# Attention with maxout FFN on one core: loads, bias, score groups and order changed

## The chip, the cores and the metric

The kernel runs on one core of a Trainium2 chip. The metric is the device time of one execution in microseconds. Engines are named as in the profile: PE is TensorE (PEld its weight loads), DVE is VectorE, ACT is ScalarE, POOL is GpSimd, SP is SyncE, whose sequencer here issues nearly all DMAs. An ending q (SPq, ACTq) means that engine's instruction queue. L12 is line 12 of the kernel before.

## The reference

Attention over 4 batches, 8 heads, 768 positions of 64 elements, with a mask and a bias, then a maxout feed-forward layer over the 3072 tokens (512 wide, hidden 768):

```
keep = (column < 8) | (0 <= row - column < 96)
dist = 96 where the column is global and not local, else |row - column|
scores = q k^T / 8 - slope[h] * dist, -1e9 where not keep;  slope[h] = 2 ** -(h + 1)
x = softmax(scores) v
out = max(x w1, x w2, x w3) w_out
```

q, k, v and the weights are fp32 in memory; the output is fp32.

## The kernel before

The 3072 tokens are 24 tiles T of 128 rows, six to a batch. A row tile only needs its own 128 positions, the 128 before it and the 8 global ones, so a tile has two sets of 128 keys (`ds`), the first tile of a batch (T = 0, 6, 12, 18) one. Inside a set, even and odd positions are split (`e`). The order of all work is written out by hand in `SCHEDULE`, a list of units; each engine executes its share of the units in that order, and an instruction waits in its engine's queue for what it needs. A unit is a letter and numbers:

- `l n.s` loads q (s = 0) or k (s = 1) of tiles 2n and 2n+1 (`load_part`, L156), 512 KB in fp32. For `short_rows` (L149; all of n >= 6, and k of n < 3) the descriptors are rows of 512 bytes in one DMA, otherwise rows of 2 KB in two DMAs of 256 KB. `v n` loads v (L171, 512-byte rows), `w`, `o` the weights.
- `c n.s.how` casts such a part to bf16 (L179); how = 0, 1, 2 is ACT, DVE, POOL. `x n.s.how` transposes it into `qkT` (L243): how 2, 3 by 8 matmuls into one PSUM tile and one copy (L282, L285), 6 to 8 by 16 small matmuls (64 rows each) into two and two copies (L261, L266/L268), 9 by DMA (L252). `C`, `Y`, `V` cast and rearrange v into the tiles `vo`, `ve`, `vf`; `G` puts the global keys into place; `Z` (L207) gathers the first key tile of a batch into `kf`.
- `S T.g.how` (L293) computes the scores of four heads g of a tile, by matmuls of 64 rows each, two row halves z side by side, into the PSUM tile `sp`, and ACT's exponential (L317) into `P`. With how = 1 (tiles 0 to 3 and one group of tile 4) the bias is added first by two matmuls of an identity with the table `bias` (L299), which `B h` prepares (L322). With how = 0 DVE multiplies `P` by the table `wmask` afterwards (`M`, L334), which `K h` prepares by ACT.
- `A T.how` multiplies P by v (L360), normalizes and writes `xb` (L373); `T T.how` transposes xb into `xT` (L376): how 0, 1 by four matmuls (L411), 6 to 8 by eight small ones (L401), 4 by DMA (L381). Twelve tiles use PE, twelve DMA.
- `F c.f.j` (L417) is one of three products of 128 hidden units for a chunk c of tokens (chunks of 4, 2, 2, 4, 4, 4, 4 tiles), four matmuls into one of three PSUM buffers `h`; j = 0 is copied by ACT (L429), j = 1, 2 are max'ed by DVE (L431, L433) into `ht`. `W`, `Q` cast the weights. `O` (L451) is the output product of a tile, `E` (L456) that of the last chunk.
- `D` (L498) issues n dummy matmuls of 512 columns (`wp`, L504): 12 before the first data, five more spread over the first 22 us.

The first k part is issued by ACT's queue before ACT's table load, the first q part by SP's (L507, L508). Two units of SP's queue are always issued in their order, so a DMA transposition that waits for `xb` holds up the loads behind it.

Of the kernel before, what the change touches and what calls it, by code (L numbers as in the profile page):

```python
# [12 lines left out]
FP32 = mybir.dt.float32  # L13
# [17 lines left out]
    T3.8 V4.2 W0.1.2 S4.1.0 D7.1 G4.0 w0.2 F0.1.0 F0.0.0 S5.1.0 c3.0.1 x3.0.6 M4.1 w1.0 W1.0.0
    S5.0.0 F0.1.1 W0.2.2 F0.1.2 v2 C2.0.0 C2.1.0 W2.0.1 F0.0.1 F0.0.2 M5.0 F0.3.0 F0.2.0 M5.1 Y2.1.1
    V5.1 F0.5.0 w1.1 W1.1.0 W2.1.1 F0.4.0 A4.1 A5.0 F0.5.1 T4.0 F0.4.1 w1.2 W1.2.0 l3.1 T5.1 F0.2.1
    F0.2.2 l4.0 c4.0.1 W2.2.0 F0.5.2 c3.1.0 x3.1.7 Z1.0 F0.4.2 F1.0.0 F1.2.0 l4.1 c4.1.1 S7.0.0
    S6.1.0 l5.0 x4.0.6 l5.1 o0 F1.0.1 F1.0.2 c5.0.1 M7.0 F1.3.0 F1.4.0 F1.4.1 o2 c5.1.1 x4.1.7
    S6.0.0 S7.1.0 G7.0 v3 F1.2.1 F1.2.2 F1.3.1 Q2.1 F0.3.1 M7.1 Q0.0 F1.5.0 F1.5.1 S8.0.0 x5.0.7
    S8.1.0 G8.1 C3.0.2 C3.1.1 Y4.0.1 F0.3.2 F1.5.2 A7.0 F1.4.2 F1.1.0 M6.0 x5.1.6 v5 o1 Q1.0 v4
    S9.0.0 S9.1.0 l7.0 l6.1 C5.0.1 C5.1.0 F1.1.1 F1.3.2 Y3.1.1 M8.0 F1.1.2 T7.0 v6 l6.0 M6.1 v7
    Y3.0.1 M9.0 O0.2.1 l7.1 C4.0.0 O0.0.0 G9.0 V8.1 A6.1 c7.0.1 M8.1 c6.1.1 x6.1.9 O0.3.0 C4.1.0
    Y4.1.1 O0.1.1 Y5.1.0 S10.1.0 T6.8 V9.1 M9.1 S10.0.0 O1.0.0 A8.1 M10.1 T8.4 F2.0.0 x7.0.9 G10.0  # L40
    F2.4.0 c6.0.0 l8.1 v9 l9.1 F2.0.1 F2.1.0 M10.0 F2.0.2 S11.0.0 c7.1.0 Y5.0.1 x6.0.6 S11.1.0 V10.1
    F2.1.1 M11.0 F2.4.1 C6.0.0 A9.0 F2.2.0 V11.1 l9.0 O1.1.1 S13.1.0 x7.1.6 S13.0.0 G13.0 M11.1
# [16 lines left out]
    O5.3.1 F6.1.1 F6.0.0 F6.0.1 F6.0.2 O5.0.1 F6.2.0 F6.2.1 F6.3.2 O5.2.0 F6.2.2 F6.1.2 F6.5.2 E
    D6.0  # L60
"""


@with_exitstack
def kernel(
# [13 lines left out]
    nc = tc.nc  # L79
# [13 lines left out]
    sizes = [4, 2, 2, 4, 4, 4, 4]  # L93
# [31 lines left out]
    rbq = persist.tile([128, 3, 128], FP32, name="rbq")  # L125
# [449 lines left out]
```

## Time and profile before

| | us |
|---|---|
| device time, median of 3 runs | 176.63 (176.61 to 176.70) |
| span of the profiled execution, first to last instruction | 174.9 |
| the profiled execution's own device time | not listed apart; the median is 1.7 above its span |
| PE / DVE / ACT / POOL busy | 169.3 / 132.5 / 120.1 / 14.3 |

A page of the profile gives busy times, the span in slices, the chain of work that ended last (followed back from the last instruction, at each step to what released it), and groups of instructions with their mean duration. The chain can also be listed in order of time: start, length, engine, output tile, line. In a table by stages each engine has its busy time and its count of instructions.

### The profile page before, as it was taken

To read this page: it belongs to the slowest core of one execution; us is meant where nothing else is said; L and a number is where in the kernel's file an instruction comes from. 1 tells how busy PE (TensorE), PEld (TensorE's weight loads), DVE (VectorE), ACT (ScalarE), POOL (GpSimd) and SP (SyncE) were. 2 spreads that over 40 slices of the span, in tenths; PEclk is the share of its full clock that TensorE was granted. 3 is DMA by queue.
4 is the path that set the end of the run, shared out by engine and by line. 5 is a ranking of instruction groups with operands and counts; after the bars stand their busy time and mean duration, and the time that the engine had idled before them with its cause. 6 is when DMAs were issued, how large, how long until landed. Compare 5 with 4: busy or idle time off the path is not lost.

```text
span 174.9 us, 4233 instructions
## 1 busy us (share of the span) xinstructions
PE 169.3 (97%) x1683; PEld 93.0 (53%) x1683; DVE 132.5 (76%) x288; ACT 120.1 (69%) x188; POOL 14.3 (8%) x25
## 2 busy tenths in 40 slices
PE   6999999999999999999999999999999999999992
PEld 2445654658684587754545545544455544444451
DVE  6668859889999999998978769995569873444510
ACT  6989999789988999999948977345594413121132
POOL 5269250000100000000000000000000000000000
PEclk9999999999999999999999999999999999999999
DMA  4999999999999999976999997563101750031205
GB/s 137 347 302 335 359 350 383 385 380 312 309 282 265 298 289 228 292 213 193 257 195 185 304 233 172 166 133 60 54 10 30 105 171 0 0 119 36 89 27 213
DMA packets 55507, 35.92 MB, mean 205 GB/s; under 512 B 18368, under 2 KB 47936, under 8 KB 55488
## 3 DMA queue, kind: packets, MB, share of 16 engines
q1 hardware_dynamic: 54304, 35.07, 73.9%
q10 hardware_dynamic: 1184, 0.59, 1.3%
q8 instruction: 13, 0.21, 0.5%
q14 instruction: 6, 0.05, 0.1%
HBM read 25.17 MB, written 6.29 MB: 180 GB/s over the span
## 4 chain that ended last, share of the span: by engine, by line
PE 94%; ACT 2%; DVE 1%; issue 1%; ACTq 0%; DVEq 0%
PE h L424 53%; PE po L439 18%; PE sp L306 7%; PE op L360 6%; PE wp L504 4%; PE tpr L261 2%; PE sp L299 2%; PE xtp L411 1%; ACT qkT L268 1%; ACT wo L496 1%; PE oph L360 1%; ACT P L317 1%; PE xtr L401 0%; PE tpp L282 0%; DVE qkT L285 0%
## 5 line engine op out<-in xcount | busy, mean ns | idle before, releaser
L424 PE MATMUL h<-xT,w 128*128 128x512 bf16 (+1 forms) x504 | 100.8, 349 | 0.0
L424 PEld LDWEIGHTS <-w 128*128 128x128 bf16 x504 | 46.7, 98 | 40.7 <-ACT w L493 0.6
L317 ACT ACTIVATE P<-sp 128x1024 bf16<-128x1024 f32 (+1 forms) x48 | 44.0, 956 | 9.2 <-PE sp L306 9.1
L429 ACT CAST h<-h 128x512 bf16<-128x512 f32 (+1 forms) x42 | 21.9, 531 | 22.1 <-PE h L424 22.1
L439 PE MATMUL po<-wo,ht 128*128 128x512 bf16 (+2 forms) x156 | 34.1, 363 | 0.0
L431 DVE TENSOR_TENSOR h<-h,h 128x512 bf16<-128x512 bf16 (+1 forms) x42 | 25.2, 605 | 10.9 <-PE h L424 8.9
L433 DVE TENSOR_TENSOR ht<-h,h 128x512 bf16<-128x512 bf16 (+1 forms) x42 | 25.5, 609 | 6.3 <-PE h L424 5.0
L334 DVE TENSOR_TENSOR P<-P,wmask 128x1024 bf16<-128x1024 bf16 x33 | 22.0, 684 | 2.0 <-ACT P L317 1.9
L439 PEld LDWEIGHTS <-ht 128*128 128x128 bf16 x156 | 14.3, 98 | 15.1 <-DVE ht L433 0.2
L448 ACT COPY ost<-po 128x512 f32<-128x512 f32 (+2 forms) x16 | 8.8, 553 | 15.8 <-PE po L439 15.3
L373 DVE TENSOR_TENSOR xb<-op,rz 128x512 bf16<-128x512 f32 x22 | 15.2, 692 | 0.8
L360 PEld LDWEIGHTS <-P 128*128 128x128 bf16 x352 | 13.4, 97 | 4.4 <-issue 0.7
L306 PE MATMUL sp<-qkT 64*128 64x128 bf16 x320 | 14.3, 218 | 0.1
L306 PEld LDWEIGHTS <-qkT 64*128 64x128 bf16 x320 | 9.3, 94 | 8.2 <-issue 5.1
L448 DVE COPY ost<-po 128x512 f32<-128x512 f32 (+1 forms) x10 | 6.5, 647 | 8.4 <-PE po L439 8.4
L188 DVE CAST qkp<-rawp 128x1024 bf16<-128x1024 f32 x12 | 8.2, 687 | 1.7 <-DMA rawp<-in_k_dram 1.6
L504 PE MATMUL wp<-zeros 128*128 128x512 bf16 x17 | 7.1, 559 | 1.5 <-DVE zeros L518 1.4
L188 ACT CAST qkp<-rawp 128x1024 bf16<-128x1024 f32 x8 | 8.4, 1050 | 0.0
L268 ACT COPY qkT<-tpr 128x512 bf16<-128x512 bf16 x12 | 6.6, 588 | 1.0 <-PE tpr L261 1.0
L268 DVE COPY qkT<-tpr 128x512 bf16<-128x512 bf16 x6 | 4.0, 688 | 3.9 <-PE tpr L261 3.9
L372 DVE RECIPROCAL rz<-op 128x8 f32<-128x8 f32 x22 | 4.4, 199 | 2.5 <-PE op L360 2.3
L360 PE MATMUL op<-vo,P 128*128 128x65 bf16 x128 | 5.4, 193 | 0.3 <-issue 0.3
(84 smaller groups left out, 127.9 us busy)
## 6 DMA issues: line engine op xcount, KB each, us to landing
rawv<-in_v_dram SPq DMA_DIRECT2D x12, 512.0 KB, 7.0
out_dram<-ost SPq DMA_DIRECT2D x23, 256.0 KB, 2.4
rawp<-in_k_dram SPq DMA_DIRECT2D x8, 512.0 KB, 5.9
rawp<-in_q_dram SPq DMA_DIRECT2D x12, 256.0 KB, 5.8
wst<-in_moe_w_dram SPq DMA_DIRECT2D x3, 1024.0 KB, 11.5
rawp<-in_q_dram SPq DMA_DIRECT2D x6, 512.0 KB, 6.2
wst<-in_moe_w_dram SPq DMA_DIRECT2D x3, 512.0 KB, 8.5
rawp<-in_k_dram SPq DMA_DIRECT2D x6, 256.0 KB, 8.6
```

The lines of the kernel that those rows point to most:

```text
L188: copies[how](qk, src)
L306: nc.tensor.matmul(sp[:, z, i, ds], k_cols(T, hsl, jp, ds), q_cols(T, hsl, jp), start=not how, stop=True, skip_group_check=True)
L317: nc.scalar.activation(dst, src, AF.Exp, bias=0.0, scale=scale)
L334: nc.vector.tensor_mul(P, P, wmask[:, g, :, 0:2])
L360: nc.tensor.matmul(o, P[:, i, ds], vs[ds][:, h], start=(ds == 0), stop=(ds == len(vs) - 1), skip_group_check=True)
L373: nc.vector.tensor_tensor(out=x.rearrange("p (g h) d -> p g h d", g=2), in0=o4[:, :, :, 0:64], in1=rz[:, :, :, None].to_broadcast([128, 2, ...
L424: nc.tensor.matmul(ps, w123[f // 2][:, dm, j, (f % 2) * 128:(f % 2) * 128 + 128], xT[c][:, dm], start=(dm == order[0]), stop=(dm == order[ ...
L429: nc.scalar.copy(h01, ps)
L431: nc.vector.tensor_max(h01s[c, f], h01s[c, f], ps)
L433: nc.vector.tensor_max(ht[c][:, f], h01s[c, f], ps)
L439: nc.tensor.matmul(po, ht[c][:, f, tt * 128:(tt + 1) * 128], wo[:, f, cols], start=(f == 0), stop=(f == NF - 1))
L448: copy(ost, po)
```

## The change

- q and k of tiles 0 to 11 all come in rows of 2 KB (`SHORT` is empty). `load_part` takes the queue: 0 SP, 1 ACT, 2 one half on each. The first k is split over SP and ACT, the first q goes by ACT, both as units of the schedule; on ACT they follow the table load and the activation `tiny`.
- The bias is added by four matmuls per group, each of an identity scaled by one head's slope (`slope_id`, prepared by `B`, seven on POOL) with one unscaled distance table `rbqb` in bf16. The group g of heads is now formed as 2i + g.
- The first tile of a batch reads its keys straight from `qkT` by two matmuls of 64 output rows each; `kf` and `Z` go.
- `U T` is both score groups of a tile; all tiles from 6 on use it.
- The v tiles are slices of one tile `vall`, whose ones are set by one memset. Casts can be split over two engines (how 3 to 5) and `Y` can copy by DMA (how 3).
- The schedule is new. In counts: of the x transpositions 11 use 16 small matmuls (13 before), 3 use eight large ones (1), 10 DMA (10); T uses PE for tiles 0 to 3 and DMA for the other 20; q/k casts on ACT/DVE/POOL and split are 3/7/11/3 (8/12/4/0), v casts 4/6/14 (10/9/5), Y and V have 23 units on POOL (4); biased score groups are 8 (9); dummies are seven at the start and five after E; of the three wo casts two are on DVE (one). Instructions: DVE 290 to 252, ACT 192 to 168, POOL 30 to 77.

The new order at its beginning, and around chunk 1:

```
D5.6 D13.1 l0.1.2 c0.1.1 l0.0.1 K5 K2 c0.0.3 x0.1.2 B7.2 B4.2 B3.1 x0.0.6 K4 B5.2 B1.2 K0 S1.1.1
B0.2 l1.1 c1.1.1 B6.2 B2.2 S1.0.1 G1.0 x1.1.3 l1.0 S0.1.1 v0 c1.0.2 x1.0.7 v1 C1.0.1 S0.0.1
...
W2.1.1 W1.1.0 A5.0 A4.1 F0.5.1 F0.2.1 w1.2 W2.2.0 F0.3.1 W1.2.2 l4.0 c4.0.5 M7.1 F0.4.1 F0.3.2
v3 U6.0 M6.0 T5.4 x4.0.7 M6.1 C3.1.1 Y3.1.1 F0.5.2 C3.0.2 Y3.0.2 F0.2.2 T4.4 A7.0 F1.0.0 A6.1
F1.1.0 F1.5.0 F1.1.1 l4.1 c4.1.2 x4.1.7 F0.4.2 U8.0 G8.0 l5.0 c5.0.2 x5.0.6 F1.5.1 F1.1.2 F1.5.2
v5 C5.0.1 F1.2.0 F1.2.1 l5.1 c5.1.5 F1.4.0 F1.4.1 F1.3.0 v4 C4.1.1 x5.1.7 o0 Q0.1 U9.0 F1.2.2
```

The code:

```diff
...
+SIZES = [4, 2, 2, 4, 4, 4, 4]
+SHORT = []
...
-    rbq = persist.tile([128, 3, 128], FP32, name="rbq")
...
     wmask = persist.tile([128, 2, 4, 3, 128], BF16, name="wmask")
-    bias = persist.tile([128, 2, 2, 2, 3, 128], BF16, name="bias")
-    vo_first = [persist.tile([128, 2 * H * 65], BF16, name=f"vof{i}") for i in range(2)]
-    vo_next = [persist.tile([128, 2 * H * 65], BF16, name=f"vo{i}") for i in range(2)]
-    ve = [persist.tile([128, 2 * H * 65], BF16, name=f"ve{i}") for i in range(2)]
-    vf = [persist.tile([128, H * 65], BF16, name=f"vf{i}") for i in range(2)]
-    kf = persist.tile([128, NP, 2, 64], BF16, name="kf")
+    rbqb = persist.tile([128, 3, 128], BF16, name="rbqb")
+    slope_id = persist.tile([128, H, 128], BF16, name="slope_id")
+    vall = persist.tile([128, 14 * H * 65], BF16, name="vall")
+    vparts = [vall[:, i * H * 65:(i + 1) * H * 65] for i in range(14)]
+    pairs = [vall[:, 2 * i * H * 65:2 * (i + 1) * H * 65] for i in range(6)]
+    vo_first, vo_next, ve, vf = pairs[0:2], pairs[2:4], pairs[4:6], vparts[12:14]
     w123 = [persist.tile([128, 4, 3, 256], BF16, name=f"w123_{i}") for i in range(3)]
...
     def heads(ap):
...
+    queues = (nc.sync, nc.scalar)
     def short_rows(n, s):
-        return n >= 6 or (s == 1 and n < 3)
+        return n >= 6 or (n, s) in SHORT
...
-    def load_part(n, s):
+    def load_part(n, s, how=0):
...
         b, t0 = divmod(2 * n, NT)
+        src = (q, k)[s][b, :, t0 * 128:(t0 + 2) * 128, :]
         r = raw_pool.tile([128, 2 * DM], FP32, name="rawp", tag="raw")
-        src = (q, k)[s][b, :, t0 * 128:(t0 + 2) * 128, :]
         if short_rows(n, s):
             r = r.rearrange("p (h x) -> p h x", h=H)
-            dma = nc.scalar if (n, s) == (0, 1) else nc.sync
-            dma.dma_start(out=r, in_=src.rearrange("h (i e) d -> i h (e d)", e=2))
+            queues[how].dma_start(out=r, in_=src.rearrange("h (i e) d -> i h (e d)", e=2))
         else:
...
             for z in range(2):
-                nc.sync.dma_start(out=r[:, z], in_=src[4 * z:4 * z + 4].rearrange("h (i e) d -> i h (e d)", e=ET))
+                queues[(how + z * (how == 2)) % 2].dma_start(out=r[:, z], in_=src[4 * z:4 * z + 4].rearrange("h (i e) d -> i h (e d)", e=ET))
         raw["p", n, s] = r
...
     def load_v(n):
...
         nc.sync.dma_start(out=r, in_=v[b, :, k * 256:k * 256 + 256, :].rearrange("h (i e) d -> i h (e d)", e=2))
...
     copies = (nc.scalar.copy, nc.vector.tensor_copy, nc.gpsimd.tensor_copy)
+    split = ((copies[0], copies[1]), (copies[1], copies[0]), (copies[2], copies[1]))
...
         qk = cast_pool.tile([128, 2 * DM], BF16, name="qkp", tag="qkb")
...
             qk = qk.rearrange("p (e z d) -> p e z d", e=ET, z=2)
...
         qb["p", n, s] = qk
+        if how >= 3:
+            for z, copy in zip(range(2), split[how - 3]):
+                if short_rows(n, s):
+                    copy(qk[:, z], src[:, z])
+                else:
+                    copy(qk[:, :, z], src[:, :, z])
+            return
         copies[how](qk, src)
...
     def same(how, dst, src):
-        if how:
+        if how >= 3:
+            queues[how - 3].dma_start(out=dst, in_=src)
+        elif how:
             copies[how](words(dst), words(src))
...
             nc.scalar.copy(dst, src)
...
         else:
...
-    def u_Z(b, how):
-        copies[how](kf.rearrange("c j e i -> c e j i"), pT(3 * b, 1)[:, :, :, 0:64])
     def batch_T(b):
...
             qkT[b] = qkT_pool.tile([128, 2, 2, NP, S // 2], BF16, name="qkT", tag="qkT")
...
         b, t = divmod(T, NT)
-        if t == 0:
-            return kf[rows, jp].rearrange("c e i -> c (e i)")
         return qkT[b][rows, 1, ds, jp, 64 * t - 64:64 * t + 64]
...
     def put_kg(T, how):
...
         sp = psS.tile([128, 2, 2, 2, 128], FP32, name="sp", tag=f"sp{g}")
...
         if how:
             for hh in range(2):
-                nc.tensor.matmul(sp[:, hh, :, 0:n], identb, bias[:, g, hh, :, sets(T)],
-                                 start=True, stop=False, skip_group_check=True)
+                for i in range(2):
+                    nc.tensor.matmul(sp[:, hh, i, 0:n], slope_id[:, 4 * hh + 2 * i + g], rbqb[:, sets(T)],
+                                     start=(i == 0), stop=False, skip_group_check=True)
         for ds in range(n):
             for i in range(2):
-                jp = 2 * g + i
+                jp = 2 * i + g
                 for z in range(2):
                     hsl = slice(64 * z, 64 * z + 64)
+                    if T % NT == 0:
+                        for e in range(2):
+                            nc.tensor.matmul(sp[64 * e:64 * e + 64, z, i, 0], qkT[T // NT][hsl, 1, e, jp, 0:64],
+                                             q_cols(T, hsl, jp), start=not how, stop=True, skip_group_check=True)
+                        continue
                     nc.tensor.matmul(sp[:, z, i, ds], k_cols(T, hsl, jp, ds), q_cols(T, hsl, jp),
...
         P = p_pool.tile([128, 4, 2, 128], BF16, name="P", tag="P")
...
             dst = P[:, :, 0].rearrange("p h (i e) -> p h i e", e=2)
...
+    def u_U(T, how):
+        for g in range(2):
+            u_S(T, g, how)
     def u_B(h, how):
-        z, g, i = h // 4, h % 4 // 2, h % 2
         mul = (nc.scalar.mul, nc.vector.tensor_scalar_mul, nc.gpsimd.tensor_scalar_mul)[how]
-        mul(bias[:, g, z, i], rbq, -slopes[h] / scale)
+        mul(slope_id[:, h], identb, -slopes[h] / scale)
...
     def u_K(h):
-        z, g, i = h // 4, h % 4 // 2, h % 2
+        z, i, g = h // 4, h % 4 // 2, h % 2
         nc.scalar.activation(wmask[:, g, 2 * z + i].rearrange("p s (i e) -> p s i e", e=2),
-                             rbq.rearrange("p s (e i) -> p s i e", e=2), AF.Exp, bias=0.0, scale=-slopes[h])
+                             rbqb.rearrange("p s (e i) -> p s i e", e=2), AF.Exp, bias=0.0, scale=-slopes[h])
...
         P = Pt[T, g]
...
         for g in range(2):
...
             for i in range(4):
-                h = 4 * (i // 2) + 2 * g + i % 2
+                h = 4 * (i // 2) + 2 * (i % 2) + g
                 y, c = (g, i) if how == 2 else (h // 4, h % 4)
...
                 for ds in range(len(vs)):
...
             if how == 2:
...
                 nc.vector.reciprocal(rz[:, g], o3[:, :, 64])
-                nc.vector.tensor_tensor(out=x.rearrange("p (z w) d -> p z w d", z=2)[:, :, 2 * g:2 * g + 2],
+                nc.vector.tensor_tensor(out=x.rearrange("p (z w y) d -> p z w y d", z=2, y=2)[:, :, :, g],
                                         in0=o3[:, :, 0:64].rearrange("p (z i) d -> p z i d", z=2),
...
                                         op=ALU.mult)
...
             nc.tensor.matmul(wp, zeros[:, 0:128], zeros, start=True, stop=True)
...
     with tc.manual_schedule():
-        load_part(0, 1)
-        load_part(0, 0)
...
+        make_identity(nc, identb)
...
+        nc.gpsimd.memset(rbqb[0:NG // 2, 0:2], float(NL))
...
-        nc.gpsimd.memset(rbq[0:NG // 2, 0:2], float(NL))
-        make_identity(nc, identb)
-        for tvar in vo_first + vo_next + ve + vf:
-            nc.vector.memset(heads(tvar)[:, :, 64:65], 1.0)
...
+        nc.vector.memset(heads(vall)[:, :, 64:65], 1.0)
...
         units = {"l": load_part, "v": load_v, "c": cast_part, "x": u_x, "w": load_w, "o": load_wo, "C": cast_v,
-                 "Y": u_Y, "Z": u_Z, "S": u_S, "M": u_M,
+                 "Y": u_Y, "S": u_S, "U": u_U, "M": u_M,
                  "A": u_A, "G": put_kg, "V": put_vg, "T": u_XT, "F": u_F1, "W": cast_w,
```

More of the change, by code (lines that the diff above doesn't have):

```diff
@@ L31 @@
[L31 to L42, printed above, removed]
@@ L506 @@
     with tc.manual_schedule():
[L507 to L508 removed]
         BIGD = 60000.0
         dist = stage_pool.tile([128, 2, 2, 64], FP32, name="dist", tag="wst0")
[L512 to L514 removed]
+        rtmp = stage_pool.tile([128, 2, 128], FP32, name="rtmp", tag="wst0")
         nc.vector.memset(shift[0:64], -128.0)
@@ L518 @@
         nc.vector.memset(zeros, 0.0)
-        near, own = rbq[:, 0:2].rearrange("p s (e i) -> p s e i", e=2), rbq[:, 2]
+        make_identity(nc, identb)
+        nc.gpsimd.iota(dist, base=128, pattern=[[-1, 2], [1, 2], [2, 64]], channel_multiplier=-2,
+                       allow_small_or_imprecise_dtypes=True)
+        near, own = rbqb[:, 0:2].rearrange("p s (e i) -> p s e i", e=2), rbqb[:, 2]
         nc.gpsimd.affine_select(out=near, in_=dist, compare_op=ALU.is_ge, fill=BIGD, base=128,
@@ L523 @@
                                 pattern=[[1, 2], [-1, 2], [-2, 64]], channel_multiplier=2)
-        nc.vector.tensor_scalar(out=own, in0=dist[:, 0].rearrange("p e i -> p (e i)"), scalar1=shift, scalar2=None, op0=ALU.add)
+        nc.gpsimd.memset(rbqb[0:NG // 2, 0:2], float(NL))
+        gap = rtmp[:, 0]
+        nc.vector.tensor_scalar(out=gap, in0=dist[:, 0].rearrange("p e i -> p (e i)"), scalar1=shift, scalar2=None, op0=ALU.add)
         nc.vector.memset(far, BIGD)
```

60 lines of the change are left out of this document (30 added, 30 removed).

## The prediction

> **What bounds the kernel now.** I read the page first, its head and the chain of work that ended last.
>
> ```profile
> span 174.9 us, 4233 instructions
> PE 169.3 (97%) x1683; PEld 93.0 (53%) x1683; DVE 132.5 (76%) x288; ACT 120.1 (69%) x188; POOL 14.3 (8%) x25
> ...
> PE 94%; ACT 2%; DVE 1%; issue 1%; ACTq 0%; DVEq 0%
> ```
>
> TensorE holds 94% of the chain, so TensorE time is what counts, and time of another engine only where TensorE waits for it. Matmul records overlap and their ends are modelled, so 97% busy is no proof; the proof is the pitch in the chain told in order of time, the second view:
>
> ```profile
> 1.40 5.30 PE wp L504 x12
> 6.70 0.83 PE tpp L282 x8
> ...
> 7.56 0.70 DVE qkT L285
> ...
> 8.30 0.59 PE wp L504 x2
> 8.90 0.43 PE sp L299 x2
> ...
> 9.36 0.40 PE sp L306 x8
> ...
> 10.30 0.33 PE sp L306 x8
> 10.63 0.28 PE tpr L261 x16
> 10.91 0.69 DVE qkT L268
> ...
> 14.74 0.22 PE sp L306 x4
> 14.96 0.32 PE wp L504
> ...
> 21.46 0.32 PE wp L504
> 21.81 1.89 PE h L424 x8
> ...
> 24.48 7.01 PE h L424 x32
> ...
> 52.28 0.22 PE xtp L411 x4
> ...
> 166.28 5.22 PE po L439 x36
> ```
>
> Each row is a start, a length and a piece of work. From 24.48 on, 32 matmuls of 512 columns take 7.01 us, 219 ns each; the final 36 run at about 145 ns because some are narrower. Between 24 and 171 us nearly every piece is a matmul. The head is different: the first 12 dummy matmuls take 442 ns each, twice the later pitch, then TensorE waits for transposed q and k (0.70 us at 7.56, 0.69 at 10.91), and dummies stand in it (1.23 us at 8.30, 14.96 and 21.46). The third view is a table of stages:
>
> ```profile
> core 0: us, PE busy (x) PEld busy (x) DVE busy (x) ACT busy (x) POOL busy (x), PEclk, DMA share, GB/s
> 8.00:11.00 3.00, 2.84 (x41) 1.41 (x39) 1.35 (x4) 2.51 (x5) 1.91 (x2) 1.00 1.21 290
> 33.00:38.00 5.00, 5.00 (x45) 2.55 (x44) 4.65 (x9) 3.82 (x5) 0.00 (x0) 1.00 1.05 384
> 8.00:22.00 14.00, 13.22 (x236) 7.63 (x235) 11.28 (x30) 12.83 (x20) 8.94 (x13) 1.00 1.14 330
> 22.00:48.00 26.00, 25.95 (x296) 15.49 (x295) 22.16 (x43) 23.36 (x40) 2.91 (x3) 1.00 1.06 353
> 48.00:111.00 63.00, 63.00 (x706) 37.42 (x705) 56.96 (x130) 53.91 (x83) 0.00 (x0) 1.00 1.01 241
> ```
>
> ScalarE is busy 12.83 of 14 us between 8 and 22, so the head is bound by TensorE and ScalarE together. From 22 to 111 VectorE (79.1 of 89 us) and ScalarE (77.3) are close behind TensorE. The DMA engines are full (share about 1.1) until 48 us.
>
> **The change part by part.** The base is the profiled execution, span 174.9 us; its own time is not listed apart. The median of the three runs, 176.63, is 1.7 above the span; I add 1.7 to each sum.
>
> *Attention output transposed by DMA.* On TensorE 12 of 24 tiles were transposed, now 4 (tiles 0 to 3). Eight pieces of 0.22 us (the row at 52.28) leave the TensorE path: **-1.8 us**. Their PSUM copies leave ScalarE and VectorE. What is late next: tiles 4 and 5 now come by DMA into a full queue.
>
> ```profile
> rawp<-in_k_dram SPq DMA_DIRECT2D x4, 256.0 KB, 8.6
> ...
> xT<-xb SPq DMA_TRANSPOSE x1, 5.0
> ```
>
> These are issue-to-landing times, loads issued between 22 and 30 us and a transpose between 60 and 70. In the new order nine pieces separate A4 from F1.0.0: seven 512-wide F units of 4 x 219 ns = 0.88, a score unit of about 0.6 and a transposition of about 0.3, that is 7.0 us. If the transpose takes 5.0, nothing is late; at 8.6 chunk 1 starts 1.6 us late. I take 0, being the nearer operation, and keep +1.6. While the transpose of tile 5 or 4 waits on SP for A's result, the loads l4.1, l5.0, v5, l5.1 and v4 stand behind it; they are used by transpositions at least 0.3 us of TensorE work later in program order only, and up to eight DMAs already in flight keep the engines fed, so 0, within the same +1.6.
>
> *Bias.* Nine score groups with bias become eight (tile 4 loses one): -0.43 (row at 8.90). Each remaining group takes four matmuls of half the columns, same columns: 0. The eight scaled copies shrink from 384 to 128 columns, seven on GpSimd before data arrive: 0 (no GpSimd row has this operation; from 0.3 to 1.0 us each, 2.1 to 7 us from 3 us on; at the upper end 0.5 late, kept). **-0.4 us.**
>
> *Tiles 0, 6, 12, 18.* Their four key copies (Z) go, off the path: 0. Their eight score groups take eight matmuls of half the output rows instead of four.
>
> ```profile
> L306 PEld LDWEIGHTS <-kf x32: 92/94/96, 11.2 to 105.7; 64*128 64x128 bf16 x32
> L208 DVE COPY kf<-qkT x2: 288/508/728, 8.3 to 97.9; 128x512 bf16<-128x512 bf16 x2
> ```
>
> If the halves run beside each other: 0. At the pace of eight ordinary ones (0.33 against 0.22): 8 x 0.11 = 0.9. If every weight load is exposed, 8 x 94 = 752 ns a group instead of 220: +4.3. I take the nearest row, **+0.9 us**.
>
> *q and k transposes.* Two units of 16 small matmuls become two of eight large ones, at the warm pitch 8 x 55 = 0.44 against 0.28: +0.3. *Units U:* the two groups already stand together in most places: 0. *Memsets, pair order, and five dummies after E:* the memsets and the order of pairs change no work of TensorE: 0. The dummies, 5 x 0.22 = 1.1 us, lie beside the last copy and store, which end later than TensorE (171.5 of 174.9): 0.
>
> *Casts.* VectorE gets 38 instructions fewer, some 17 us at its mean of 132.5/288 = 0.46; ScalarE 24 fewer, 15 us at 0.64; GpSimd 47 more, 27 us at 0.57. A wait in the body shows what this can return:
>
> ```profile
> 42.76 1.06 ACT qkT L268 x2
> ...
> 45.34 0.94 ACT wo L496
> ...
> 46.61 0.39 PE tpr L261 x15
> ```
>
> The chain leaves TensorE from 42.76 to 46.61, but beside it TensorE does real work, in the order of time:
>
> ```profile
> 42.98 3.23 PE L424 MATMUL h<-xT,w 128*128 128x256 bf16 x24
> ```
>
> At half of 219 ns these 24 are 2.6 us of the 3.9, and a score group is 0.4, so 0.9 us at most is lost. Now two of three `wo` casts are VectorE's: **-0.6 us** (0 to -0.9).
>
> *The head.* Loading in 2-KB rows and from two queues:
>
> ```profile
> 0.73 2.59 SPq L168 DMA_DIRECT2D rawp<-in_q_dram  x4
> 1.19 1.28 ACT L517 ACT_TABLE_LOAD   x1 [1.19 <-PEq L556]
> 2.48 0.20 ACT L517 ACTIVATE tiny<-shift 128x1 f32<-128x1 f32 x1
> 3.37 0.59 SPq L164 DMA_DIRECT2D rawp<-in_k_dram  x1
> 4.00 3.55 SPq L175 DMA_DIRECT2D rawv<-in_v_dram  x2
> 6.41 0.69 DVE L188 CAST qkp<-rawp 128x1024 bf16<-128x1024 f32 x1 [0.16 <-DMA rawp<-in_q_dram]
> ...
> 7.83 1.04 POOL L188 CAST qkp<-rawp 128x1024 bf16<-128x1024 f32 x1 [4.66 <-DMA rawp<-in_q_dram]
> ```
>
> The loads issued at 3.37 and 4.00 have 512-byte rows; in the window 8 to 11, theirs, the engines give 290 GB/s at a DMA share of 1.21; from 33 to 38, 2-KB rows give 384 at 1.05. Three k loads of 0.52 MB: 5.4 us becomes 4.1, 1.3 us of DMA time. But the first q now follows the table load and `tiny` on ScalarE's queue. Issues of 0.65 us each: before, q0 was issued from 0.73 to 2.03 and cast at 6.41. If the issues wait for the activation (0.8 + 1.28 + 0.20 = 2.3), k0's second half and q0 end at 4.25, 2.2 later; if they do not, at 2.75, 0.7 later. Against that: k1 is on chip early, so the wait at 10.91 goes (-0.7); q0's cast is halved over two engines (-0.3); the 1.2 us of dummies leave. ScalarE, still full, loses four bias scalings, a v copy and a weight cast, but gets the 1024-wide copies of x0.1 and x2.1. I add: q0 +1.4 (middle of 0.7 and 2.2), k1 -0.7, cast -0.3, dummies -0.6 (half, since ScalarE is full beside them) and ScalarE's copies +0.2: **0.0 us**, from -2.0 to +2.5.
>
> The Trainium skill's "DMA: Bandwidth & Descriptors" (Specifications) gives 512 bytes as the size from which a transfer reaches line rate; by it the 2-KB rows save nothing instead of 1.3 us of DMA time. The trace disagrees, 290 against 384 GB/s. The same page (Rules for kernel authors) says several issuing engines share the same DMA engines and save only issue time; no run here shows two queues of equal loads, and by it the second queue would be worth at most three issues of 0.65 us.
>
> **Sum:** -1.8 - 0.4 + 0.9 + 0.3 - 0.6 + 0.0 = **-1.6 us**, span 173.3, time **175.0 us**.
>
> **The rivals.**
> 1. *Cold head (slower).* Before, TensorE worked without a break from 1.40 to 7.5 us, and the pitch halves only between 7.5 and 8.9 (442 ns, then 295). Now seven dummies end at about 1.4 + 7 x 0.44 = 4.5, and TensorE idles until k0 is cast. If the fast pitch needs some 5.3 us of unbroken work, it comes only that long after the first scores at about 9.4. Half of those 5.3 us is lost, +2.7: **177.7**; if it holds until the F units, work of 12 us stretched with ScalarE beside it, up to +5. It decides from the point at which matmuls after 9 us still keep 0.4 us per 512 columns. For it: the dummies are fewer and the gap longer. Against: the granted clock reads 1.00 throughout (so it can't tell), and ScalarE hides part. The Trainium skill, "TensorE: Matmul & The Clock Gate" (Part 1: The HAM clock gate) has the clock halved until about 3.4 us of sustained work and again after an idle window as long; the trace agrees with the halving, and took 6 us.
> 2. *Everything overlaps (faster).* The ScalarE queue issues at once, the halves run beside each other, and the head starts 2 us sooner: 175.0 - 2.0 - 0.9 = **172.1**. For it: VectorE and ScalarE, which are unloaded, were above 85% busy from 22 to 111. Against: TensorE waits for them rarely in the chain.
> 3. *GpSimd slows VectorE.* The kf copy took 728 ns at 8.3 us, with GpSimd's cast of 7.83 beside it, and 288 at 97.9, without. About 27 us more GpSimd work could stretch VectorE's copies by 0.44 us each; VectorE has some 14 such copies left, 6 us, less than the 17 it sheds. If those fall on the path one time in three: +2, **177.0**.
> 4. *Late DMA transposes:* +1.6, **176.6**: no difference.
>
> 5. *It does not do what it says:* the loads are not what TensorE waits for, so 2-KB rows and the second queue change nothing; this leaves the sum as it is without k1's 0.7: 175.7, inside the forecast.
>
> **How the numbers follow.** Forecast (and 5) 0.45; cold head 0.22; everything overlaps 0.18; GpSimd 0.07; late transposes 0.08. The forecast's own range is 173.5 to 176.3. The range of all, 172.0 to 179.0, reaches over rivals 1 to 4 and leaves out the deep ends (exposed weight loads, cold until F). About 0.2%, 0.35 us, is what a measurement of this kernel can tell from no change: faster 0.45 + 0.18 less 0.03 for the forecast's slow end = 0.60; same 0.08 (rival 4); slower 0.22 + 0.07 + 0.03 = 0.32.
>
> **What would show it.** In the changed profile's chain: wp x7 at about 440 ns and the next 512-column pitch; the first score group at about 9.4 us; the first F piece at about 22; score pieces of tiles 6, 12, 18 at 0.33 or 0.22 per eight; no chain piece of ScalarE between 30 and 50; XT transposes landing 5 us or later, with F1.0.0 directly behind. The forecast is wrong if the pitch after 9 us is the slow one, or if the F units stop for `xT` or for the drains of `h`.

## The result: 192.6 us, 8.1% slower

| | median, us | runs | against before |
|---|---|---|---|
| before | 176.66 | 176.61 to 176.78 | |
| after | 192.57 | 189.79 to 192.72 | 1.0814 [1.0738, 1.0891] |

The forecast was 175.0, at most 179.0. The runs of the changed kernel and of the experiments made from it spread by up to 4% (those of the kernel before by 0.4% at most), so medians here are over all runs and ratios over those within 1.5% of a kernel's fastest (8.1% is 14.4 us, where the medians differ by 15.9), and the profiled executions of e1_t_pe, e10_q0_only and e11_warm_only are not among these. The profiled execution of the changed kernel took 192.45 us. Its page has:

```profile
span 190.7 us, 4220 instructions
PE 168.3 (88%) x1638; PEld 93.5 (49%) x1660; DVE 129.6 (68%) x250; ACT 103.0 (54%) x162; POOL 50.3 (26%) x72
...
PE 43%; DMA 20%; issue 4%; DVE 4%; POOL 3%; ACT 3%; SPq 2%; POOLq 0%; ACTq 0%; DVEq 0%
```

22 matmul records are missing here (1638 against 1660 weight loads); e2_loads_first below, with the same TensorE instructions in the same order and all records, has 168.7 us. So TensorE is busy for about 0.6 us less than the 169.3 before. The span less that is TensorE's idle time: 22.0 us, where it was 5.6. That is all of the loss, and a fifth of the chain is now DMA. The table by stages says where (columns as in the prediction: each engine's busy time, then the granted clock, the DMA share and GB/s):

```profile
core 0: us, PE busy (x) PEld busy (x) DVE busy (x) ACT busy (x) POOL busy (x), PEclk, DMA share, GB/s
8.00:15.00 7.00, 5.41 (x66) 3.52 (x68) 3.10 (x5) 4.11 (x7) 3.68 (x6) 0.53 1.10 339
...
30.00:40.00 10.00, 9.06 (x95) 4.81 (x96) 10.00 (x15) 7.13 (x13) 3.38 (x4) 1.00 0.61 202
40.00:50.00 10.00, 9.79 (x115) 5.82 (x118) 9.80 (x22) 4.25 (x10) 2.51 (x4) 1.00 0.57 157
50.00:60.00 10.00, 7.99 (x114) 6.16 (x114) 7.51 (x15) 7.58 (x14) 5.21 (x7) 1.00 1.13 255
...
80.00:100.00 20.00, 16.24 (x175) 9.13 (x177) 12.47 (x28) 12.75 (x18) 4.04 (x6) 1.00 1.09 241
```

The same view of the kernel before:

```profile
30.00:40.00 10.00, 10.00 (x123) 5.85 (x121) 8.87 (x17) 8.23 (x14) 0.00 (x0) 1.00 1.04 375
40.00:50.00 10.00, 9.96 (x149) 7.46 (x144) 9.41 (x21) 9.08 (x16) 0.62 (x1) 1.00 1.09 308
```

Three things differ. Up to 30 us TensorE idles for about 9 us (2.2 in the kernel before), and from 8.5 to 15 us its clock is half. From 30 to 50 the loads run at about half the rate, while TensorE idles for only 1.2 us. After 50 it idles for some 12 us (3.4 before). So a part of the loss lies ahead of the gap in the loads, and the larger part behind it. SP's rows in order of time, and the wait that its queue names, explain the gap:

```profile
24.99 2.75 SPq L169 DMA_DIRECT2D rawp<-in_q_dram  x2
27.83 0.54 SPq L176 DMA_DIRECT2D rawv<-in_v_dram  x1
40.91 2.61 SPq L395 DMA_TRANSPOSE xT<-xb  x2
43.57 1.23 SPq L169 DMA_DIRECT2D rawp<-in_k_dram  x2
```

```profile
SPq L395 <- DVE xb L387: 13.3, 1, 13.3
```

After v3 at 27.83 the next issue is tile 5's transpose, and it waits 13.3 us for `xb`. Everything behind it (l4.1, l5.0, v5, l5.1, v4) comes that much later. Long after that the chain still stands on loads and DMA transposes (that this comes from the gap is argued here; e1 and e2 below test it):

```profile
57.83 10.09 DMA rawp<-in_k_dram
...
72.68 4.58 DMA rawv<-in_v_dram
...
85.66 4.16 DMA xT<-xb
```

### The profile page after: what moved, and what is told of

Read it like the earlier page. It is cut to its first block, busy times and chain, and to the rows that moved or that the text cites. A ratio compares the mean times of both kernels' runs of the same rounds, so it can differ in the third digit from the quotient of the medians.

```text
span 190.7 us, 4220 instructions
## 1 busy us (share of the span) xinstructions
PE 168.3 (88%) x1638; PEld 93.5 (49%) x1660; DVE 129.6 (68%) x250; ACT 103.0 (54%) x162; POOL 50.3 (26%) x72
## 4 chain that ended last, share of the span: by engine, by line
PE 43%; DMA 20%; issue 4%; DVE 4%; POOL 3%; ACT 3%; SPq 2%; POOLq 0%; ACTq 0%; DVEq 0%
PE h L438 30%; DMA xT<-xb 9%; PE po L453 8%; DMA rawv<-in_v_dram 6%; DMA rawp<-in_k_dram 5%; PE op L374 2%; PE sp L317 1%; POOL qkp L197 1%; POOL vall L206 1%; POOL vall L200 1%; DVE P L348 1%; SPq L463 1%; ACT vall L200 1%; DVE xb L387 1%; DVE h L445 1%
## 5 line engine op out<-in xcount | busy, mean ns | idle before, releaser
L438 PE MATMUL h<-xT,w 128*128 128x512 bf16 (+1 forms) x490 | 98.8, 348 | 6.1 <-DMA xT<-xb 2.3
L328 ACT ACTIVATE P<-sp 128x1024 bf16<-128x1024 f32 (+1 forms) x48 | 43.6, 956 | 19.0 <-PE sp L317 14.4
L197 POOL CAST qkp<-rawp 128x1024 bf16<-128x1024 f32 x11 | 12.9, 1190 | 51.7 <-DMA rawp<-in_k_dram 46.0
L462 ACT COPY ost<-po 128x512 f32<-128x512 f32 (+2 forms) x19 | 10.6, 561 | 25.6 <-PE po L453 18.4
L206 POOL COPY vall<-vall 4x520 int32<-4x520 int32 (+2 forms) x23 | 15.6, 685 | 22.6 <-ACT vall L208 10.2
L453 PEld LDWEIGHTS <-ht 128*128 128x128 bf16 x156 | 14.2, 98 | 14.7 <-issue 0.2
L387 DVE TENSOR_TENSOR xb<-op,rz 128x512 bf16<-128x512 f32 x19 | 13.1, 692 | 1.1 <-DMA xT<-xb 0.5
L200 POOL CAST vall<-rawv 128x512 bf16<-128x512 f32 x14 | 8.5, 615 | 14.0 <-DMA rawv<-in_v_dram 13.8
L374 PE MATMUL op<-vall,P 128*128 128x65 bf16 x288 | 11.4, 193 | 0.8 <-POOL vall L206 0.4
L267 PE MATMUL tpr<-identb,qkp 64*128 64x64 bf16 x176 | 4.9, 199 | 6.5 <-DVE slope_id L336 3.4
L462 DVE COPY ost<-po 128x512 f32<-128x512 f32 (+1 forms) x7 | 4.4, 633 | 7.9 <-PE po L453 7.8
L267 PEld LDWEIGHTS <-qkp 64*128 64x128 bf16 x176 | 3.7, 100 | 8.4 <-issue 4.1
L208 ACT COPY vall<-vall 64x1040 bf16<-64x1040 bf16 (+2 forms) x7 | 6.5, 934 | 1.7 <-POOL vall L200 1.6
```

Source lines behind the costliest of these rows:

```text
L206: copies[how](words(dst), words(src))
L328: nc.scalar.activation(dst, src, AF.Exp, bias=0.0, scale=scale)
L374: nc.tensor.matmul(o, P[:, i, ds], vs[ds][:, h], start=(ds == 0), stop=(ds == len(vs) - 1), skip_group_check=True)
L387: nc.vector.tensor_tensor(out=x.rearrange("p (g h) d -> p g h d", g=2), in0=o4[:, :, :, 0:64], in1=rz[:, :, :, None].to_broadcast([128, 2, ...
L438: nc.tensor.matmul(ps, w123[f // 2][:, dm, j, (f % 2) * 128:(f % 2) * 128 + 128], xT[c][:, dm], start=(dm == order[0]), stop=(dm == order[ ...
L453: nc.tensor.matmul(po, ht[c][:, f, tt * 128:(tt + 1) * 128], wo[:, f, cols], start=(f == 0), stop=(f == NF - 1))
```

## The experiments

Names beginning with b start from the kernel before and add one part of the change; names beginning with e start from the changed kernel and undo a part. Each is compared with runs of the kernel before on the same chip (medians 176.7 to 176.8). The last column is what the ratio makes of that median; the gains and losses named below are differences of this column. Most intervals are 0.6 to 0.9 us to either side (1.3 for the changed kernel).

| kernel | median, us | ratio to before | us over before |
|---|---|---|---|
| the changed kernel | 192.57 | 1.0814 [1.0738, 1.0891] | 14.4 |
| b1_t_dma | 191.36 | 1.0834 [1.0797, 1.0871] | 14.7 |
| b4_t_dma_w12 | 191.79 | 1.0840 [1.0809, 1.0871] | 14.9 |
| b5_t_late | 184.25 | 1.0421 [1.0377, 1.0464] | 7.4 |
| b3_casts | 178.53 | 1.0086 [1.0054, 1.0119] | 1.5 |
| b2_rows | 177.37 | 1.0026 [1.0016, 1.0036] | 0.5 |
| b6_code | 177.20 | 1.0023 [1.0014, 1.0032] | 0.4 |
| b7_code_fewer_d | 177.31 | 1.0029 [1.0020, 1.0039] | 0.5 |
| e1_t_pe | 187.76 | 1.0598 [1.0542, 1.0655] | 10.6 |
| e2_loads_first | 188.14 | 1.0629 [1.0565, 1.0692] | 11.1 |
| e4_head | 184.90 | 1.0429 [1.0381, 1.0478] | 7.6 |
| e10_q0_only | 187.48 | 1.0482 [1.0455, 1.0509] | 8.5 |
| e11_warm_only | 190.60 | none; runs 186.6 to 194.4 | none |
| e5_head_loads | 189.67 | 1.0703 [1.0645, 1.0762] | 12.4 |
| e6_all_loads | 203.99 | 1.1548 [1.1519, 1.1577] | 27.4 |
| e9_head_t4 | 182.21 | 1.0310 [1.0255, 1.0366] | 5.5 |
| e8_head_t8 | 185.72 | 1.0495 [1.0433, 1.0558] | 8.8 |
| e7_two_casts | 191.27 | 1.0852 [1.0801, 1.0904] | 15.1 |
| e3_no_pool_casts | 215.81 | 1.2178 [1.2127, 1.2228] | 38.5 |

### The DMA transposes

**e1_t_pe**

```diff
-T5.4 ... T4.4 ... T6.4 ... T7.4
+T5.1 ... T4.0 ... T6.8 ... T7.0
```

> The changed kernel, but the transposes of tiles 4 to 7 back on TensorE, as before. Theory Q (their DMAs wait at the head of SP's queue, 13.3 us for tile 5, and hold the loads l4.1, l5.0, v5, l5.1, v4 behind them; TensorE later waits for those): 192.6 less 5 to 9 plus some 1.5 us of TensorE work, 184 to 189 us, and the issue gap on SP at 28 to 41 us gone. Theory P (GpSimd's casts that hold VectorE are the cost): 191 to 194.5, since the casts stay.

3.8 us less than the changed kernel: theory Q's direction, at the small end of its range (184 to 189; the median is 187.76). The gap at 28 us went, but the next transpose by DMA, of k of tile 12 (`x6.1.9`), took its place in SP's rows:

```profile
49.48 1.54 SPq L165 DMA_DIRECT2D rawp<-in_k_dram  x1
61.69 1.33 SPq L258 DMA_TRANSPOSE qkT<-qkp  x1
```

**e2_loads_first**

```diff
-v3 U6.0 M6.0 T5.4
+v3 l4.1 l5.0 v5 l5.1 v4 o0 U6.0 M6.0 T5.4
```

> The changed kernel with all its DMA transposes, but l4.1, l5.0, v5, l5.1, v4 and o0 issued behind v3, ahead of the transpose of tile 5. Theory Q: the loads no longer stand behind the wait, so 184 to 189 us, DMA share in 30 to 50 us back to about 1. Rival Q2 (the DMA transposes are themselves what TensorE waits for, being late at tiles 4 to 7): unchanged within 1.5 us. Theory P: unchanged too.

188.14, as Q says, with every transpose still a DMA and the DMA share from 30 to 40 us back at 1.05. So the loads behind the wait cost 3.3 us. It is not the whole.

**e5_head_loads, e6_all_loads** add e4's head (below) to e2; e6 also moves later loads:

```diff
-l4.0 c4.0.5 ... v3 U6.0 M6.0 T5.4
+l4.0 v3 v5 v4 l4.1 l5.0 l5.1 l6.0 c4.0.5 l6.1 ... U6.0 M6.0 T5.4
```

> The changed kernel with the head of e4_head (both halves of q0 over two queues, 6 more warm-up matmuls) and the loads of e2_loads_first (six loads ahead of the transpose of tile 5). If the two losses were independent (7.7 and 4.4 us), 180.5 us. Theory HQ (they are one loss told twice: a later TensorE makes tile 5's xb later, and that lengthens the wait that holds the loads; e4_head's wait is 6.5 us where it was 13.3): less than the sum, 182 to 184.

> As e5_head_loads, but every load of q, k and v from l4.0 on stands in SP's order right behind the cast that frees its buffer, ahead of the waits of all later DMA transposes that it can pass. Theory Q: what is left over the kernel before is loads held behind other waiting DMA transposes (q and k of tiles 12 on, and tiles 8 on): 177 to 180. Rival: a wait for a buffer now holds the transposes instead, or the loads come early enough already: 181 to 185.

Both ranges were missed, in both runs. e5 is 4.8 slower than e4, which doesn't have those loads ahead, and e6 is slowest but one of all. TensorE's waits for `xT` (sum, times, longest), of e5 and then of e6:

```profile
PE h L438 <- DMA xT<-xb: 5.8, 2, 5.3
```

```profile
PE h L438 <- DMA xT<-xb: 13.7, 4, 11.1
```

In e6 SP issues eight loads between 35.6 and 43.6 us and then the transposes; its chain has

```profile
37.30 4.75 DMA rawp<-in_k_dram
...
47.06 4.75 DMA xT<-xb
```

Put behind the loads, the transpose itself is late: its issue waits in the queue and its packets land 4.75 us after the issue. Put ahead of them, it holds the loads. None of the places tried in this queue was free of both. Transposes and loads on different queues, which would take the holding alone away, were not tried.

**b1_t_dma, b4_t_dma_w12, b5_t_late** ask for the price alone, in the old order:

```diff
-T4.0 F0.4.1 w1.2 W1.2.0 l3.1 T5.1 ... T7.0 ... T6.8
+T4.4 F0.4.1 w1.2 W1.2.0 l3.1 T5.4 ... T7.4 ... T6.4        (b1)
+w1.2 T4.4 F0.4.1 W1.2.0 l3.1 T5.4 ... T7.4 ... T6.4        (b4)
-T11.0 ... T9.8 ... T10.6 ... T15.8
+T11.4 ... T9.4 ... T10.4 ... T15.4                         (b5)
```

> The kernel before, with one part of the change alone: the transposes of tiles 4 to 7 by DMA at the places where TensorE did them. The prediction's step (0.6 us saved on TensorE, nothing lost) gives 176.2. Theory Q: the waits at the head of SP's queue hold l4.0, l4.1, l5.0, l5.1, v3 and TensorE waits for them: 178 to 183.

> The kernel before with the transposes of tiles 4 to 7 by DMA, as b1_t_dma, but the load of weights w1.2 ahead of tile 4's on SP, so that no weights stand behind the wait. Theory D (loads of q, k and v behind the wait, and transposes behind bytes): 179 to 187, less than b1_t_dma's 191.4 by the 5.8 us for which TensorE waited for those weights. Rival (the weights were all of it): 176 to 177.5.

> The kernel before with the other four transposes that the change moves (tiles 9, 10, 11, 15) by DMA, 4 to 7 left on TensorE. By the prediction's step, four transposes of TensorE less (0.15 us each): 175.8 to 176.4. Theory D (loads are still streaming until about 100 us): 177.5 to 182.

Four transposes alone cost 14.7 us, far outside the range. b4 misses both of its ranges too: TensorE no longer waits 5.8 us for weights, but the time is the same (14.9). What TensorE waits for in b4:

```profile
PE h L424 <- DMA xT<-xb: 6.9, 1, 6.9
PE tpr L261 <- ACT qkp L188: 2.6, 1, 2.6
```

So the weights were not the reason. One wait is for a load of q or k held behind the first transpose, the longer one for a transpose that is itself late (issued at 70.26, behind stores and another transpose). The last four cost 7.4 us by themselves, at the upper end of theory D's range. b4 on SP, and by stages:

```profile
17.22 6.88 SPq L483 DMA_DIRECT2D wst<-in_moe_w_dram  x2
33.17 1.29 SPq L381 DMA_TRANSPOSE xT<-xb  x1
34.51 1.23 SPq L168 DMA_DIRECT2D rawp<-in_k_dram  x2
```

```profile
30.00:40.00 10.00, 7.40 (x77) 3.89 (x76) 6.15 (x12) 5.64 (x7) 0.00 (x0) 1.00 0.61 177
40.00:50.00 10.00, 8.50 (x92) 5.76 (x93) 6.17 (x11) 5.65 (x12) 0.00 (x0) 0.66 0.97 312
...
60.00:80.00 20.00, 13.07 (x125) 7.85 (x124) 11.12 (x25) 9.92 (x18) 0.00 (x0) 0.83 1.08 261
```

SP stands for nine microseconds (24.1 to 33.2), the engines' share falls to 0.61, and TensorE idles 2.6 and 1.5 us of the two stretches of ten shown, then 6.9 between 60 and 80 in the wait for `xT`. Each long idle comes with a lower clock (0.66, 0.83), so the loss is counted twice: of the 15.6 us that the span grew, 4.3 are TensorE's busy time (173.6 against 169.3). In b5, where 6.2 us are one wait of TensorE for an `xT`, the chain holds two transposes behind streaming loads, five microseconds each:

```profile
76.65 5.08 DMA xT<-xb
...
102.01 5.33 DMA xT<-xb
```

### The head

**e4_head, e10_q0_only, e11_warm_only**: e4 has both edits, e10 the first, e11 the other two.

```diff
-l0.0.1
+l0.0.2
-D5.6 ... x0.1.2
+D5.8 ... x0.1.2 D0.4
```

> The changed kernel, but the two loads of q0 over the two queues, as those of k0 are, and 6 more warm-up matmuls, 2 at the start and 4 behind the transposes of k0. Theory H (first F unit 3.8 us later than before because q0 lands at 9.0 and the clock is cold until 15): first F unit 1.5 to 3 us earlier, and the same off the end, 189.5 to 191. Rival: the stall of the loads swallows it, because it is set by data and not by TensorE's start: 192 to 193.

> The changed kernel with one half of e4_head: q0's loads over two queues, no more warm-up matmuls. Theory H1 (q0's landing at 9.0 us is what the head lost): 184.5 to 187. Theory H2 (the cold clock is): 190 to 193.

> The changed kernel with the other half of e4_head: 6 more warm-up matmuls, q0 as in the change. H1: 190 to 193. H2: 185 to 188. Where both are needed, each alone gives 188 to 191.

e4 gives back 6.8 us, more than twice what was expected of it. e10 alone gives back 5.9, which is inside H1's range. e11's four runs reach from 186.6 to 194.4 us and decide nothing. The order of time in the changed kernel, then in e4:

```profile
5.60 0.62 PE L288 MATMUL tpp<-identb,qkp 128*128 128x128 bf16 x8 [1.04 <-DVE qkp L197]
...
9.01 0.43 DVE L195 CAST qkp<-rawp 128x512 bf16<-128x512 f32 x1 [3.47 <-DMA rawp<-in_q_dram]
...
9.59 0.61 PE L267 MATMUL tpr<-identb,qkp 64*128 64x64 bf16 x16 [3.37 <-DVE slope_id L336]
10.13 1.03 PE L305 MATMUL sp<-rbqb,slope_id 128*128 128x256 bf16 x4
...
25.64 1.89 PE L438 MATMUL h<-xT,w 128*128 128x512 bf16 x7
```

```profile
6.71 0.43 DVE L195 CAST qkp<-rawp 128x512 bf16<-128x512 f32 x1 [1.24 <-DMA rawp<-in_q_dram]
...
7.62 0.61 PE L305 MATMUL sp<-rbqb,slope_id 128*128 128x256 bf16 x4
...
21.37 1.89 PE L438 MATMUL h<-xT,w 128*128 128x512 bf16 x8 [0.52 <-POOL vall L206]
```

q0's second half is cast 2.3 us earlier, the four bias matmuls take 0.61 and not 1.03 us, and the first F unit begins at 21.4, not 25.6. (The `slope_id` that TensorE's 3.37 us are put down to is the instruction right behind that cast on VectorE.) In the profiled executions of the two halves F begins at 24.8 (e10) and at 25.5 (e11).

The two hang together. In the changed kernel TensorE had the fast pitch at 5.60, where eight transposes took 0.62 us, and lost it in the 3.4 us of waiting for q0: the granted clock reads 1.00 up to 8.5 us and 0.50 from there to 15. In e1_t_pe, which begins in the same way, those transposes took 1.04 us and the bias matmuls 1.03 us: the fast pitch had not come yet, and the granted clock still reads 1.00 there. So a fall of the clock shows in that column, a clock that has not risen yet shows only in the pitch. The clock in e11:

```profile
8.00:10.00 2.00, 0.26 (x16) 0.29 (x16) 0.53 (x2) 0.20 (x1) 0.00 (x0) 1.00 1.10 363
10.00:12.00 2.00, 1.75 (x27) 0.98 (x18) 1.80 (x2) 1.84 (x4) 1.04 (x1) 0.88 1.22 301
12.00:14.00 2.00, 2.00 (x25) 1.57 (x24) 0.50 (x2) 1.71 (x3) 1.58 (x3) 0.50 1.06 340
```

Warmed up, TensorE waits 2.7 us for q0 (7.0 to 9.7), and two microseconds later the clock is halved in spite of the work. In e4 the waits there are 0.3 and 0.5 us, and it stays at 1.00. So more warm-up without an earlier q0 did not hold the clock in this execution. Whether the clock falls differs between executions of one kernel: its mean over the span is 0.982 to 0.991 in all four of the changed kernel and 0.999 or 1.000 in all four of e4, but 1.000 in five of e10's six and in one of e11's four. The times follow it only in part (e10's five at 1.000 reach from 185.2 to 190.2 us), so it does not settle how the 6.8 us divide.

F begins 4.3 us earlier in e4, and its profiled execution ends 8.1 earlier (182.6 and 190.7 us of span). Where the other 3.8 us can come from, SP's row and wait show:

```profile
33.87 2.59 SPq L395 DMA_TRANSPOSE xT<-xb  x2
```

```profile
SPq L395 <- DVE xb L387: 6.5, 1, 6.5
```

Tile 5's `xb` is ready 7.0 us earlier than in the changed kernel (40.91), and the loads are held 6.5 us, not 13.3. The stall was longer where what stands ahead of it came later; no run changes the one without the other.

### Both together

**e9_head_t4** is e4 and e1 in one; **e8_head_t8** also has

```diff
-T9.4 ... T10.4 ... T11.4 ... T15.4
+T9.8 ... T10.6 ... T11.0 ... T15.8
```

> The changed kernel with the head of e4_head and all eight transposes that the change moved from TensorE to DMA (tiles 4 to 7, 9, 10, 11, 15) back on TensorE. Theory D (a DMA transpose among the loads costs on both sides: it holds them while it waits, and stands behind their bytes when it does not): TensorE idles as little as before from 30 us on, 176.5 to 180. Rival: GpSimd's casts and the new order keep it above 181.

> As e8_head_t8, but only tiles 4 to 7 back on TensorE. Theory D: the transposes of tiles 9, 10, 11, 15 still stand among the loads of q, k and v up to about 110 us; 1 to 4 us above e8_head_t8. Rival (only the first stall matters): within 1 us of it.

e9 takes back 8.9 of the 14.4 us. e8 was expected to be better and is 3.3 worse: in the new order T stands directly behind the unit that makes its `xb`, a place that suits a DMA; TensorE, in order, now waits there. One such wait is about half of it:

```profile
PE xtr L415 <- DVE xb L387: 1.6, 1, 1.6
```

So e8 doesn't tell what the late transposes cost in the new order; b5 tells it for the old one.

What is left in e9 can be seen, though no run takes it away. TensorE idles for about 3.0 us between 22 and 60 us, and from 22 to 40 VectorE is busy 17.6 of 18 us there (14.7 in the kernel before). It idles for 2.2 more between 80 and 100, where the chain has a load of v, issued at 87.77, that landed 5.7 us later.

### The casts

**e3_no_pool_casts**: 32 units `c`, `C`, `W` with how 2 get 0, those with 5 get 3. **e7_two_casts** and **b3_casts**:

```diff
-W0.0.2 ... W2.0.2
+W0.0.0 ... W2.0.0                                       (e7)
-W0.0.0 ... c3.0.1 C2.1.0 W2.0.1 W1.2.0 c4.0.1 ...
+W0.0.2 ... c3.0.2 C2.1.2 W2.0.2 W1.2.2 c4.0.2 ...       (b3, 24 units)
```

> The changed kernel, but all casts of q, k, v and weights that GpSimd did (30 whole ones, 2 halves) on ScalarE. Theory P: the 2.98 us copies of qkT on VectorE go back to 0.17 us and the time falls by 4 to 8 us, to 184.5 to 188.5. Theory Q: VectorE's long copies go, but the loads still come late, 190 to 194 us; ScalarE's added 25 us may cost some of it.

> The changed kernel, but the first and the fourth cast of weights (W0.0 and W2.0) on ScalarE and not GpSimd; nothing else is moved. Theory P (GpSimd's back-to-back casts of 1024 elements hold VectorE's copy of qkT for 2.98 us): that copy takes 0.2 us or about 1, S4 and S5 start some 1 to 2 us earlier, 189 to 191.5. Rival: ScalarE's own queue delays exponentials by as much: 192 to 194.

> The kernel before, with one part of the change alone: the 24 casts that the change moves to GpSimd are done there (where the change splits one in halves, the whole one). The prediction's step: 0 to 0.9 us saved, 176 to 176.8. Theory P (GpSimd's casts hold VectorE, and are themselves slower): 178 to 184.

The copy of `qkT` and GpSimd's casts beside it, in the changed kernel and in e7:

```profile
25.56 3.00 POOL L507 CAST w<-wst 128x1024 bf16<-128x1024 f32 x3
25.62 2.98 DVE L239 COPY qkT<-qkT 128x32 bf16<-128x32 bf16 x1
...
28.66 0.62 PE L317 MATMUL sp<-qkT 64*128 64x128 bf16 x16 [1.12 <-DVE qkT L239]
```

```profile
25.64 2.02 POOL L507 CAST w<-wst 128x1024 bf16<-128x1024 f32 x2
25.70 1.99 DVE L239 COPY qkT<-qkT 128x32 bf16<-128x32 bf16 x1
```

With three casts the copy takes 2.98 us, with two 1.99; in e3, with none, 0.17. It is no single case: the changed kernel's six copies of this kind take 833 ns on average, 169 in e3, and VectorE's two casts of weights 1389, 691 in e3. So GpSimd's casts do hold VectorE. What that is worth is not shown: by the medians e7 is 1.3 us faster than the changed kernel, by the ratios 0.7 slower, and the intervals overlap. e3 doesn't tell either. The casts, in ScalarE's order now, held up what TensorE and VectorE needed, and with that SP's stall grew:

```profile
27.84 0.54 SPq L176 DMA_DIRECT2D rawv<-in_v_dram  x1
52.67 2.60 SPq L395 DMA_TRANSPOSE xT<-xb  x2
```

25 us of queue now instead of 13, and 215.8 us. b3 is the clean answer: the casts on GpSimd cost 1.5 us in the old order (1.0 to 2.1), just under theory P's range.

### Rows and computation

**b2_rows**; **b6_code** is the changed kernel's code with the old schedule and `SHORT = [(0, 1), (1, 1), (2, 1)]`; **b7_code_fewer_d** leaves out D1.1, D9.2, D3.1, D7.1 as well.

```diff
-        return n >= 6 or (s == 1 and n < 3)
+        return n >= 6
...
-                nc.sync.dma_start(out=r[:, z], ...
+                (nc.scalar if (n, s, z) == (0, 1, 1) else nc.sync).dma_start(out=r[:, z], ...
```

> The kernel before, with one part of the change alone: k of tiles 0 to 5 in 2-KB rows, the first two loads of k0 over two queues, with TensorE's transposes of the form that goes with that. The prediction's steps (head 0.0, from -2.0 to +2.5, with q0 1.4 later and k1 0.7 earlier; transposes +0.3): 176 to 178. Rival (2-KB rows bring every early load forward): 174.5 to 176.

> The changed kernel's code with the order, the rows, the queues, the casts and the transposes of the kernel before (its Z units left out, since nothing reads their copies; the units of biases and masks renumbered to the new pairing of heads). What is left of the change: bias by scaled identities, half-row scores of first tiles, one memset of v's ones. The prediction's steps (-0.4 and +0.9, from 0 to +4.3): 177.3. Rival (the half-row matmuls cost no more than the copies that they replace): 176.2 to 176.8.

> As b6_code, without the four single warm-up units D1.1, D9.2, D3.1, D7.1 (5 matmuls of 0.2 to 0.6 us) that stand among the first scores. If TensorE's work is what counts there: 1.0 to 1.5 us under b6_code, and perhaps under the kernel before. Rival (they fill waits for data): the same as b6_code within 0.4.

177.37, 177.20, 177.31: these parts cost 0.5 and 0.4 us, and five dummies fewer bring nothing. No version tried beats the kernel before.

## Why the prediction was wrong, step by step

Two steps failed, and each alone is enough to leave the range of all, 172.0 to 179.0: with the first undone (e1) the time is 10.6 us over before, with the second undone (e4) 7.6.

- *Attention output by DMA (-1.8, with +1.6 kept): the loads behind a waiting transpose, put at 0.* TensorE's busy time did fall, by about 0.6 us in all. "Up to eight DMAs already in flight keep the engines fed, so 0" did not hold: the wait was 13.3 us, what was in flight ran out, and the share fell to 0.61 and 0.57. In the old order the four early transposes cost 14.7 to 14.9 us alone and the four late ones 7.4. In the new order taking the early four back returns 3.8 (e1), or 2.1 where the head is mended already (e4 to e9). These sizes don't add up to one price, since the price hangs on what stands ahead of the transposes and behind them. The landing was nearly right: 5.0 taken, 3.7 in the median of the 20, 2.4 to 6.9 in all. The prediction named the queue's order, but gave the lateness of the transposes a price (rival 4) and the loads behind them none.
- *The head (0.0, from -2.0 to +2.5):* F began 3.8 us later, and e4 returns 6.8 us at the end (5.1 from e1 to e9). ScalarE's queue did issue at once, as rival 2 had it (q0's halves at 1.64 and 2.36), but both halves stood one behind the other on it, and the second was cast at 9.01, where q0 was cast at 6.41 before: +2.6, where +1.4 was allowed. Rival 1, the cold head, has its sign: four matmuls of 256 columns in 1.03 us at 10.13 is the slow pitch. Its mechanism (too few dummies, so that the fast pitch comes late) is what e1_t_pe shows; in the changed kernel's own trace the fast pitch was there at 5.60 and was lost in the wait for q0. Its 2.7 us is near what the trace gives: 5.41 busy us at a clock of 0.53 are some 2.5 us more than at full clock, by estimate. No run has this alone.
- *Casts (-0.6):* wrong sign, +1.5 in b3. Rival 3 named the mechanism (728 against 288 ns); one copy was held 2.8 us. The relief of VectorE, some 17 us, hardly came: its busy time fell by 2.9 us, from 132.5 to 129.6, and from 30 to 40 us it is busy 10.00 of 10. The mean that the 17 were taken from was too high for the instructions that went, and those that GpSimd holds became longer.
- *Bias and first tiles (-0.4, +0.9):* the sum, +0.5, is what b6 gives (0.4), but by luck. The two row halves run beside each other, as rival 2 had it: in the changed kernel's chain 16 of them, two groups, take 0.35 us, where eight ordinary matmuls took 0.33 before, so this term is about 0.1 and not 0.9.

```profile
44.59 0.35 PE sp L314 x16
```

- *q and k transposes, rows (+0.3):* right within its error, +0.5 in b2 with the head of that kernel.
- *U, memsets, dummies after E (0):* nothing against it. From the last F2 matmul to the end of the span it is 3.4 us in both kernels.

b2, b3 and b6 add up to 2.4 us; e9 is 5.5 above the kernel before. The other 3.1 us are open: the late transposes in the new places, the casts on GpSimd in the new order and the order itself were not told apart.

## What to carry to other kernels

A DMA that waits for a computed tile has two prices on an in-order queue that also carries loads: what stands behind it while it waits, and its own landing behind their bytes when it doesn't. Count both before an operation of 0.2 us is taken off a busy TensorE; in all versions tried here, with the DMA engines full, the operation was the cheaper one. Such a queue can make an earlier delay longer: in the profiled executions here 4.3 us at the first F unit were 8.1 at the end. And a wait for the first operand can cost the clock as well, so the two are to be counted together.

## What the runs showed of the hardware

- A VectorE copy of 128x32 bf16, 0.17 us alone, lasted to the end of a row of GpSimd casts: 1.99 us for two, 2.98 for three. The Trainium skill, "SBUF — State Buffer" (Terms), says that the two engines share a port pair by an exclusive lock, held for the full instruction. The trace agrees on the blocking, but here the copy did not get in between one cast and the next.
- TensorE's granted clock fell from 1.00 to 0.50 some 2.3 us into a wait in the changed kernel (idle from 6.2 us, clock down from 8.5) and after a wait of 2.7 us in e11, and stayed up over waits of 0.3 and 0.5 us in e4. The Trainium skill, "TensorE: Matmul & The Clock Gate" (Part 1: The HAM clock gate), asks for an idle window of about 3.4 us; here it fell after less.
- The granted clock reads 1.00 also where TensorE has not come up to the fast pitch yet: in e1_t_pe four matmuls of 256 columns take 1.03 us at a reading of 1.00, in e4 0.61. The rows of the kernel before in the prediction have the same: its first dummies take 442 ns each, matmuls of the same width later 219, at a reading of 1.00 throughout.
